# Slot weights split by ACT and by POOL in halves, the seventh batch's stored from ACT's queue, g loaded later, the stores of w_out's rows spread out

## The chip, the cores and the metric

The kernel runs on one core of one Trainium2 chip. The core has five engines with a queue each: PE (matrix products), ACT (functions, copies out of PSUM), DVE (vector work), POOL (vector work, SBUF only) and SP (here it only issues DMAs; ACT issues one too). Each takes its instructions strictly in order. The metric is the device time of one execution in microseconds, and lower is better: the median of the runs of before is 1417.61 us (1417.1 to 1418.57).

## What is computed

Three layers follow one another on x of shape (8, 3072, 256), all in float32: a spectral layer per batch, a mixture with soft slots over all 24576 tokens, and a SoLU block.

```python
X = np.fft.rfft(x, axis=1)
Yr = Xr @ w_r - Xi @ w_i + b_r                  # Yi likewise
Yr = np.sign(Yr) * np.maximum(np.abs(Yr) - lam, 0.0)
y = np.fft.irfft(Yr + 1j * Yi, n=3072, axis=1)

logits = y @ phi                                # 32 slots
d = softmax over the tokens;  c = softmax over the slots
slot_input = d.T @ y
slot_out[e] = np.maximum(slot_input[e] @ w1[e], 0.0) @ w2[e]
x2 = c @ slot_out

h = x2 @ w_in
solu = h * softmax(h)
ln = (solu - mean) / np.sqrt(var + 1e-6) * g_ln
out = ln @ w_out
```

w_in and w_out arrive as float64; the kernel decodes their 64-bit words itself.

## The kernel before

**First phase (0 to about 612 us).** `phase1` works batch by batch, the batches counted here from 1 to 8 (b = 0 to 7 in the code). A batch is 12 steps (`for i in range(B * NT)`, 96 in all, about 6 us each). A step holds one or two `stage1` (a product over 96 rows; its input is split into a high part by ACT, L237, and a low part by POOL, L238), one `stage2` (`xps`), one `mix` (`pb`, `pa`, then three DVE operations, the last of them L345, and a subtraction on POOL, L346) and one `st_transpose` (`sps`). Between them run the small operations of the batch before, which turn its spectrum into logits and softmax weights: `qt`, `qtr`, `e2`, `r_x`, `inv1`, `ltr` (which writes the logits to `lg_sb`, L459), `maxt`, `maxb`, `fwd1`, `dtr`, `d_x`, `fwd2`, `slots`.

**What sets the order.** A heap of delayed calls: `after(n, f, ...)` runs f n calls of `tick()` later (four ticks to a step). The numbers stand in the table `LAG`. What a call issues goes to the in-order queues at that place.

**Slot weights.** `csoft` to `c_x` make the weights c of a batch, `ct_sb` (96 x 1024, transposed by DVE at L536). `c_out` splits them: POOL copies the high part to `ct_h` (L551), then subtracts to get the low part in place in `ct_sb` (L552). `c_store` (L557) sends both to `c_dram` from SP's queue. The second phase reads them back. Batch 8 is stored unsplit, from ACT's queue (L548). `ct_sb` and the next batch's `lg_sb` share one buffer (tag `sc`), so `ltr` of batch b+1 has to wait until `ct_sb` of batch b has been stored.

**Decoding.** `dec_step` runs once a step from i = 2 on, with one small piece of work each time: a load of a raw block, eight DVE operations on it (L668 to L675), then for w_in one store to `win_dram`, for w_out a scaling by g on ACT (`dec_scale`, L698) and in one more step all the stores of the block's rows (`dec_rows`: 2 stores for the first two blocks, 8 for the last two). `load_g` closes the list and loads w_out back as `wo`.

**End of the first phase.** When batch 8's last `qt` is due, the buffers of the loop are released and `load_w` puts 15 loads of 512 KB (`wt`, w1 and w2) and one of 1 MB (`wi`) into SP's queue (L115, L123, L1200). Then the rest of the heap runs: `qt` to `slots` of batch 8, and `c_store` of batch 7.

**Second phase (from about 612 us).** `phase2` first computes the slots' outputs (`ph`, `h1`, `po`, `psl`, `pg`), then 192 tiles of 128 tokens, bounded by PE.

**DMA semaphores.** Each DMA has one of eight semaphores, in turn over both queues (`DMAHW0` to `DMAHW7` in the rows below); a DMA waits until the DMA that had its semaphore before has landed. So eight are under way at most.

Of the kernel before, what the change touches and what calls it, by code (L numbers as in the profile page):

```python
# [8 lines left out]
F32 = mybir.dt.float32  # L9
# [4 lines left out]
AF = mybir.ActivationFunctionType  # L14
# [6 lines left out]

LAG = dict(
    csoft_last=5, csoft2_last=4, csoft3_last=4, c_x_last=12, head=4, split0=3, load_x=3, a_out=0, qt=5, qtr=3, e2=3, r_x=2, inv1=3, mx=0, ltr=1, maxt=2, maxb=4,
    dsub=0, dexp=2, csoft=5, fwd1=4, rescale=3, rexp=3, csoft2=3, csoft3=5, c_x=4, c_out=1, c_store=5, dtr=3, d_x=3, fwd2=4,
    sums4=0, slots=1, sums=4,
)

# [8 lines left out]
def kernel(  # L36
# [112 lines left out]
    def phase1(pl: ExitStack, pr_: ExitStack):  # L149
# [39 lines left out]
        def after(dq, fn, *a):  # L189
            heapq.heappush(heap, (now[0] + dq, now[1], fn, a))  # L190
            now[1] += 1
# [353 lines left out]
        def c_out(b, ct):  # L545
            f = ct.rearrange("p n j -> p (n j)")
            if b == B - 1:
                ACT.dma_start(out=c_dram[b, 0].rearrange("h s x -> (h s) x"), in_=f.bitcast(F32))  # L548
                return
            ch = sm_p.tile([96, 1024], F32R, name="ct_h", tag="c_sb")  # L550
            POOL.tensor_copy(out=ch, in_=f.bitcast(F32))  # L551
            POOL.tensor_tensor(out=f, in0=f.bitcast(F32), in1=ch.bitcast(F32), op=ALU.subtract)  # L552
            after(LAG["c_store"], c_store, b, ch, f)

        def c_store(b, ch, f):
            for k, z in enumerate((ch, f)):
                SP.dma_start(out=c_dram[b, k].rearrange("h s x -> (h s) x"), in_=z.bitcast(F32))  # L557

        def fwd1(b, h):
            if h == 0:  # L560
# [96 lines left out]
        def decode(src, dst, k):  # L657
            z = g_p.tile([128, 2048], I32, name="dec", tag="wo")
            raw, a, c = z[:, 0:1024].bitcast(I64), z[:, 1024:1536], z[:, 1536:2048]
            m = g_p.tile([128, 512], I32, name="dm", tag="dm")  # L660
            v = z[:, 0:1024].rearrange("p (n two) -> p n two", two=2)
            hi = v[:, :, 1]
            lo = z[:, 0:1024].bitcast(U32).rearrange("p (n two) -> p n two", two=2)[:, :, 0]
            r = raw if len(src.shape) == 2 else raw.rearrange("p (k d) -> p k d", k=2)
            SP.dma_start(out=r, in_=src)
            f = a.bitcast(F32) if len(src.shape) == 2 else a.bitcast(F32).rearrange("p (k d) -> p k d", k=2)
            dec_ops.extend([
                lambda: DVE.tensor_scalar(out=a, in0=hi, scalar1=3, scalar2=0x7FFFFFF8, op0=ALU.logical_shift_left, op1=ALU.bitwise_and),  # L668
                lambda: DVE.scalar_tensor_tensor(out=a, in0=hi, scalar=_s32(0x80000000), in1=a, op0=ALU.bitwise_and, op1=ALU.bitwise_or),
                lambda: DVE.tensor_scalar(out=c, in0=hi, scalar1=0x7FF00000, scalar2=None, op0=ALU.bitwise_and),  # L670
                lambda: DVE.tensor_scalar(out=m, in0=c, scalar1=float(0x38100000), scalar2=-1.0, op0=ALU.is_ge, op1=ALU.mult),
                lambda: DVE.scalar_tensor_tensor(out=a, in0=a, scalar=0x40000000, in1=m, op0=ALU.bitwise_xor, op1=ALU.bitwise_and),
                lambda: DVE.tensor_scalar(out=c, in0=a, scalar1=_s32(0xFF800000), scalar2=None, op0=ALU.bitwise_and),
                lambda: DVE.scalar_tensor_tensor(out=c.bitcast(F32), in0=lo, scalar=2.0**-52, in1=c.bitcast(F32), op0=ALU.mult, op1=ALU.mult),
                lambda: DVE.tensor_tensor(out=a.bitcast(F32), in0=c.bitcast(F32), in1=a.bitcast(F32), op=ALU.add),  # L675
            ])
            if k < 0:
                dec_ops.append(lambda: dec_out(dst, f))
            else:
                dec_ops.append(lambda: dec_scale(f, k))  # L680
                dec_ops.append(lambda: dec_rows(f, k))

        def dec_step():
            if dec_ops:
                dec_ops.pop(0)()
            elif decs:
                decode(*decs.pop(0))
                if not decs:
                    dec_ops.append(load_g)

# [6 lines left out]
            for n in range(2):  # L697
                ACT.activation(out=f[:, n, :], in_=f[:, n, :], func=AF.Copy, scale=gl[:, k + n:k + n + 1])  # L698

        def dec_rows(f, k):  # L700
            for n in range(k, k + 2):
                if n < MA:
                    SP.dma_start(out=wout_dram[128 * n:128 * n + 128], in_=f[:, n - k, :])
                    continue
                v = wout_dram[128 * MA:1024].rearrange("(i b c) d -> b c i d", b=4, c=MB)
                for c in range(4):
                    SP.dma_start(out=v[n - MA, c], in_=f[32 * c:32 * c + 32, n - k, :])


        dft = sm_p.tile([96, 96], F32, name="dft", tag="qt_sb", bufs=2)  # L710
# [13 lines left out]
        def weights():  # L724
# [28 lines left out]
            26: (f_sb[:, 16:32, :], c_f[:, 16:32, :]),  # L753
            30: (w2_sb, c_w2),
            31: (sel, c_sel),
            33: (gl, g_ln.rearrange("(k p) -> p k", p=128)),
        }

        def load_const(o, i):
# [48 lines left out]
        for i in range(B * NT):  # L808
# [3 lines left out]
            tick()  # L812
            if i + 1 < B * NT:
                stage2(*divmod(i + 1, NT))
                if i > 1:
                    dec_step()
                if t % 2 == 0:
                    k = i // 2 + 2
                    bb, r = divmod(k, 6)
# [504 lines left out]
```

## Time and profile before

| | us |
|---|---|
| median of 3 runs | 1417.61 (1417.1 to 1418.57) |
| the profiled execution, device time | 1420.87 |
| its span, first to last instruction | 1419.1 |
| PE busy in the span | 1332.3 (94%) |
| DVE, ACT, POOL busy | 1219.3, 1040.8, 938.6 |
| mean granted PE clock | 0.975 |

The span is 1.8 us shorter than the profiled execution, and that execution is 3.3 us above the median of the runs. The page cuts the span into 40 slices: PE is busy 9 tenths or more in nearly all of them, except in the first slice and around 600 to 700 us. The averages over the span say little: the first phase, the passage at its end and the second phase have different limits.

### The profile page before, as it was taken

The numbers are of one execution on the slowest core, as the hardware profiler recorded it, in microseconds if no ns is written. First come the engines' busy times: TensorE is split into PE (matmuls) and PEld (weight loads), VectorE is DVE, ScalarE is ACT, GpSimd is POOL, SyncE is SP. The second block draws the span as 40 slices with busy tenths as digits, with TensorE's granted clock in tenths as the row PEclk, the third lists the DMA queues.
The fourth block names the chain that finished last, engine by engine and source line by source line (L and its number), as shares of the span: only waits on it lengthen the run. The fifth ranks groups of instructions, "written<-read, shape, count | busy, mean of one in ns | idle before, by whom it ended". The sixth has DMA issues, their size and how long they took to land.

```text
span 1419.1 us, 28550 instructions
## 1 busy us (share of the span) xinstructions
PE 1332.3 (94%) x10012; PEld 1133.4 (80%) x10012; DVE 1219.3 (86%) x1885; ACT 1040.8 (73%) x1999; POOL 938.6 (66%) x963
## 2 busy tenths in 40 slices
PE   6999999999999898937699999999999999999998
PEld 3888888888888787714588888888888888888787
DVE  6767989898988798815799999999999999999985
ACT  5557565657565664413599999999999999999886
POOL 5546575757574743301278878788787887879996
PEclk8899999999999999968799999999999999999999
DMA  9965364737273653274256665666656665566552
GB/s 271 291 177 169 112 194 120 212 101 208 85 208 101 190 179 105 88 283 132 81 186 207 199 189 187 200 208 198 189 189 198 206 202 187 189 198 206 167 177 83
DMA packets 207774, 250.84 MB, mean 177 GB/s; under 512 B 15536, under 2 KB 148400, under 8 KB 207632
## 3 DMA queue, kind: packets, MB, share of 16 engines
q1 hardware_dynamic: 207520, 248.63, 56.3%
q8 instruction: 80, 1.31, 0.4%
q14 instruction: 62, 0.51, 0.1%
q10 hardware_dynamic: 112, 0.39, 0.1%
HBM read 141.09 MB, written 107.87 MB: 175 GB/s over the span
## 4 chain that ended last, share of the span: by engine, by line
PE 67%; DVE 11%; POOL 9%; DMA 5%; issue 4%; ACT 2%; SPq 1%; POOLq 0%; DVEq 0%; ACTq 0%
PE po L89 33%; PE pb L89 6%; PE hps L89 6%; PE pu L92 5%; PE pm L89 4%; PE s L89 4%; PE xps L89 4%; DMA xc<-in_x_dram 3%; PE pa L89 3%; PE sps L92 2%; POOL x L238 2%; POOL ul L1080 1%; DMA c_dram<-ct_sb 1%; DVE yb L343 1%; DVE dm_sb L591 1%
## 5 line engine op out<-in xcount | busy, mean ns | idle before, releaser
L89 PE MATMUL po<-gw,uh 128*128 128x512 f32 x1536 | 407.1, 406 | 3.8 <-POOL uh L1079 3.7
L89 PEld LDWEIGHTS po<-gw,uh 128*128 128x128 f32 x1536 | 274.5, 189 | 57.5 <-POOL uh L1079 6.4
L346 POOL TENSOR_TENSOR s<-yb,s 128x512 f32<-128x512 f32 x95 | 132.0, 1389 | 205.3 <-DVE s L345 186.1
L998 DVE TENSOR_REDUCE st<-hps 128x1 f32<-128x1024 f32 x192 | 235.1, 1225 | 29.8 <-PE hps L89 10.4
L1080 POOL TENSOR_TENSOR ul<-t,uh 128x512 fp32r<-128x512 f32 x189 | 244.8, 1295 | 15.2
L1013 DVE SCALAR_TENSOR_TENSOR u<-hps,e 128x1024 f32<-128x1024 f32 x192 | 233.2, 1214 | 1.3 <-ACT e L1005 1.3
L89 PEld LDWEIGHTS po<-gw,ul 128*128 128x128 f32 x1536 | 207.4, 188 | 17.7
L1088 ACT ACTIVATE sq<-u,st 128x1024 f32<-128x1024 f32 x192 | 219.5, 1143 | 0.0
L1005 ACT ACTIVATE e<-hps,st 128x1024 f32<-128x1024 f32 x192 | 214.2, 1116 | 2.9 <-DVE st L998 2.9
L89 PE MATMUL po<-gw,ul 128*128 128x256 f32 x1536 | 210.4, 279 | 0.0
L1079 POOL CAST uh<-t 128x512 fp32r<-128x512 f32 x189 | 116.0, 614 | 135.6 <-DMA t<-td 102.3
L238 POOL TENSOR_TENSOR x<-xc,x 96x512 fp32r<-96x512 f32 x120 | 165.3, 1385 | 38.0 <-ACT x L237 36.0
L1061 ACT ACTIVATE uh<-pu 128x512 fp32r<-128x512 f32 x195 | 116.8, 599 | 66.8 <-PE pu L92 56.6
L1129 ACT ACTIVATE osb<-po,st 128x512 f32<-128x512 f32 x192 | 130.7, 681 | 9.6 <-PE po L89 6.9
L1070 DVE TENSOR_TENSOR ul<-pu,uh 128x512 fp32r<-128x512 f32 x195 | 133.6, 686 | 3.6 <-ACT uh L1061 3.6
L1042 DVE STREAM_TRANSPOSE tb<-u 128x512 f32<-128x512 f32 x189 | 132.6, 702 | 0.0
L264 ACT ACTIVATE asb<-s 96x512 f32<-96x512 f32 x112 | 66.7, 595 | 80.7 <-PE s L89 80.7
L89 PE MATMUL s<-x,df_h 96*96 96x512 f32 x240 | 105.2, 440 | 17.7 <-POOL x L238 7.0
L92 PEld LDWEIGHTS pu<-ident,u 128*128 128x128 f32 x768 | 96.5, 141 | 26.0 <-issue 0.8
L92 PE MATMUL pu<-ident,u 128*128 128x128 f32 x768 | 116.6, 275 | 0.0
L89 PE MATMUL hps<-gst,ct 128*128 128x512 f32 x336 | 106.8, 400 | 10.0 <-DVE u L1013 8.6
L1136 POOL TENSOR_TENSOR os<-osb 128x1024 f32<-128x1024 f32 x47 | 113.4, 2413 | 0.0
(205 smaller groups left out, 2593.1 us busy)
## 6 DMA issues: line engine op xcount, KB each, us to landing
td<-tb SPq DMA_DIRECT2D x189, 256.0 KB, 2.1
t<-td SPq DMA_DIRECT2D x189, 256.0 KB, 3.0
apt<-ad SPq DMA_DIRECT2D x96, 256.0 KB, 3.9
out_dram<-os SPq DMA_DIRECT2D x47, 512.0 KB, 3.7
xc<-in_x_dram SPq DMA_DIRECT2D x56, 384.0 KB, 4.0
ad<-asb SPq DMA_DIRECT2D x56, 384.0 KB, 3.6
ct<-c_dram SPq DMA_DIRECT2D x96, 128.0 KB, 3.4
wt<-in_moe_w_dram SPq DMA_DIRECT2D x21, 512.0 KB, 8.5
```

The source lines that it names most:

```text
L89: PE.matmul(out=out, lhsT=lhsT, rhs=rhs, start=start, stop=stop)
L92: PE.transpose(out=out, in_=in_, identity=ident[0:k, 0:k])
L238: POOL.tensor_tensor(out=lo, in0=t, in1=hi.bitcast(F32), op=ALU.subtract)
L346: (DVE if (b, t) == (B - 1, NT - 1) else POOL).tensor_tensor(out=s, in0=yb, in1=s, op=ALU.subtract)
L998: DVE.tensor_reduce(out=st[:, 0, k:k + 1], in_=hps[i], op=ALU.min, axis=AX.X)
L1005: ACT.activation(out=e, in_=hps[i], func=AF.Exp, bias=st[:, 0, k:k + 1], scale=-1.0, accum_out=st[:, 1, k:k + 1])
L1013: DVE.scalar_tensor_tensor(out=u, in0=hps.pop(i), scalar=1.0, in1=et.pop(i), op0=ALU.mult, op1=ALU.mult, accum_out=st[:, 2, k:k + 1])
L1042: DVE.transpose(out=t, in_=v)
L1070: DVE.tensor_tensor(out=ul[:, z, :], in0=ut.pop((i, n)), in1=uht[i][0][:, z, :].bitcast(F32), op=ALU.subtract)
L1080: POOL.tensor_tensor(out=ul[:, MA:8, :].rearrange("p c (a j) -> p c a j", a=4), in0=v, in1=w.bitcast(F32), op=ALU.subtract)
L1088: ACT.activation(out=sq, in_=ut.pop(i), func=AF.Square, bias=st[:, 2, k:k + 1], scale=-float(DFF), accum_out=st[:, 3, k:k + 1])
L1129: ACT.activation(out=o[:, k], in_=pot.pop(i), func=AF.Copy, scale=stt[j][:, 4, k:k + 1])
```

## The change

`c_out` moves the copy of the high part from POOL to ACT, one tick later (`c_out` 1 to 2). The subtraction is cut into two halves of 512 columns, two and four ticks after that (`c_lo`), and the stores come three ticks behind the second half. The stores of batch 7 are issued by ACT instead of SP. g (`gl`) is no longer loaded among the early constants but when the last block of w_in is taken up. `dec_rows` does one row block or half of one at a time, so the 20 row stores of w_out lie in 12 steps instead of 4; `dec_step` starts at i = 0 instead of 2.

```diff
-    ... c_out=1, c_store=5, ...
+    ... c_out=2, c_lo=2, c_store=3, ...
...
-            POOL.tensor_copy(out=ch, in_=f.bitcast(F32))
-            POOL.tensor_tensor(out=f, in0=f.bitcast(F32), in1=ch.bitcast(F32), op=ALU.subtract)
-            after(LAG["c_store"], c_store, b, ch, f)
+            ACT.activation(out=ch, in_=f.bitcast(F32), func=AF.Copy)
+            after(LAG["c_lo"], c_lo, b, ch, f, 0)
+            after(LAG["c_lo"] + 2, c_lo, b, ch, f, 1)
+
+        def c_lo(b, ch, f, z):
+            z_ = slice(512 * z, 512 * z + 512)
+            POOL.tensor_tensor(out=f[:, z_], in0=f[:, z_].bitcast(F32), in1=ch[:, z_].bitcast(F32), op=ALU.subtract)
+            if z:
+                after(LAG["c_store"], c_store, b, ch, f)
...
-                SP.dma_start(out=c_dram[b, k].rearrange("h s x -> (h s) x"), in_=z.bitcast(F32))
+                (ACT if b == B - 2 else SP).dma_start(out=c_dram[b, k].rearrange("h s x -> (h s) x"), in_=z.bitcast(F32))
...
-                dec_ops.append(lambda: dec_rows(f, k))
+                for n in range(k, k + 2):
+                    for q in range(0, 4, 2 if n >= MA else 4):
+                        dec_ops.append(lambda n=n, q=q: dec_rows(f, k, n, q))
...
                 decode(*decs.pop(0))
+                if len(decs) == 4:
+                    SP.dma_start(out=gl, in_=g_ln.rearrange("(k p) -> p k", p=128))
...
-            33: (gl, g_ln.rearrange("(k p) -> p k", p=128)),
...
-                if i > 1:
-                    dec_step()
+                dec_step()
```

ACT's queue at the end of the first phase, before. Names are out<-in; in brackets stand the semaphores that the instruction waits for. `qt_sb`, `q_sb`, `r_sb`, `lt_sb`, `lg_sb` are batch 8's.

```order
L397 ACTIVATE q_sb<-pm 128x256 [waits PE_49]
L358 ACTIVATE st<-sps 128x512 [waits PE_49] x2
L413 ACTIVATE r_sb<-pm 128x256 [waits PE_49]
L385 ACTIVATE qt_sb<-pm 128x2x2x64 [waits PE_49]
L397 ACTIVATE q_sb<-pm 128x256 [waits PE_49]
L413 ACTIVATE r_sb<-pm 128x256 [waits PE_49]
L440 ACTIVATE lt_sb<-pm 128x384 [waits PE_49] x2
L459 ACTIVATE lg_sb<-pm 96x512 [waits DVE_49,DMAHW3_49,PE_49,Pool_49]
```

The same place of ACT's queue now.

```order
L397 ACTIVATE q_sb<-pm 128x256 [waits PE_49]
L551 ACTIVATE ct_h<-ct_sb 96x1024 [waits DVE_49,Pool_49]
L358 ACTIVATE st<-sps 128x512 [waits PE_49] x2
L413 ACTIVATE r_sb<-pm 128x256 [waits PE_49]
L385 ACTIVATE qt_sb<-pm 128x2x2x64 [waits PE_49]
L563 DMA c_dram<-ct_h 96x1024 [waits DMAHW3_49,Activation_49]
L563 DMA c_dram<-ct_sb 96x1024 [waits DMAHW5_49,Pool_49]
L397 ACTIVATE q_sb<-pm 128x256 [waits PE_49]
L413 ACTIVATE r_sb<-pm 128x256 [waits PE_49]
L440 ACTIVATE lt_sb<-pm 128x384 [waits PE_49] x2
L459 ACTIVATE lg_sb<-pm 96x512 [waits DMAHW5_49,PE_49]
```

The copy and the two stores of batch 7 now stand in ACT's queue ahead of batch 8's `q_sb`, and `lg_sb` waits for the second of these stores.

SP's queue in the same stretch, before: the end of the loads of `load_w`, then the stores.

```order
L123 DMA wt<-in_moe_w_dram 128x4x256 [waits DMAHW7_49]
L123 DMA wt<-in_moe_w_dram 128x4x256 [waits DMAHW0_49]
L1200 DMA wi<-win_dram 128x2x1024 [waits DMAHW1_49]
L557 DMA c_dram<-ct_h 96x1024 [waits DMAHW2_49,Pool_49]
L557 DMA c_dram<-ct_sb 96x1024 [waits DMAHW3_49,Pool_49]
L123 DMA ws<-in_moe_w_dram 128x2x256 [waits DMAHW4_49,PE_49]
```

SP's queue now, from the first load of `load_w`; the semaphores 3 and 5 that are missing between 2, 4 and 6 went to the two stores on ACT.

```order
L115 DMA wt<-in_moe_w_dram 128x1024 [waits DVE_49,PE_49,DMAHW2_49,Activation_49,Pool_49]
L115 DMA wt<-in_moe_w_dram 128x1024 [waits DMAHW4_49]
L115 DMA wt<-in_moe_w_dram 128x1024 [waits DMAHW6_49]
L115 DMA wt<-in_moe_w_dram 128x1024 [waits DMAHW7_49]
L115 DMA wt<-in_moe_w_dram 128x1024 [waits DMAHW0_49]
L115 DMA wt<-in_moe_w_dram 128x1024 [waits DMAHW1_49]
L115 DMA wt<-in_moe_w_dram 128x1024 [waits DMAHW2_49]
L115 DMA wt<-in_moe_w_dram 128x1024 [waits DMAHW3_49]
L115 DMA wt<-in_moe_w_dram 128x1024 [waits DMAHW4_49]
L115 DMA wt<-in_moe_w_dram 128x1024 [waits DMAHW5_49]
```

Of the loads, the eighth now waits for the landing of the first store, the tenth for that of the second.

POOL's queue where batch 1's weights are split, before (the same in batches 2 to 5).

```order
L346 TENSOR_TENSOR s<-yb,s 128x512
L238 TENSOR_TENSOR x_2298<-xc,x_2298 96x512
L551 CAST ct_h<-ct_sb 96x1024
L552 TENSOR_TENSOR ct_sb<-ct_sb,ct_h 96x1024
L238 TENSOR_TENSOR x_2329<-xc,x_2329 96x512
L346 TENSOR_TENSOR s<-yb,s 128x512
L238 TENSOR_TENSOR x_2386<-xc,x_2386 96x512
```

POOL's queue there now.

```order
L346 TENSOR_TENSOR s<-yb,s 128x512
L238 TENSOR_TENSOR x_2299<-xc,x_2299 96x512
L238 TENSOR_TENSOR x_2327<-xc,x_2327 96x512
L346 TENSOR_TENSOR s<-yb,s 128x512
L238 TENSOR_TENSOR x_2386<-xc,x_2386 96x512
L557 TENSOR_TENSOR ct_sb<-ct_sb,ct_h 96x512
L238 TENSOR_TENSOR x_2413<-xc,x_2413 96x512
L557 TENSOR_TENSOR ct_sb<-ct_sb,ct_h 96x512
```

The copy is gone from POOL, and the halves of the subtraction stand one input split (L238) apart, behind two of them that they stood ahead of. For batches 6 and 7 no L238 is left there, and the two halves follow each other directly.

## Rows read from the trace of the kernel before

**Rows 1.** Windows: stretch, us, busy time of each engine, PEclk, DMA share, GB/s.
```profile
200.00:250.00 50.00, 48.66 (x519) 41.24 (x518) 45.73 (x83) 30.73 (x69) 29.16 (x22) 1.00 0.42 123
...
600.00:640.00 40.00, 14.15 (x138) 9.95 (x136) 10.35 (x14) 5.67 (x12) 5.00 (x4) 0.70 0.77 278
...
620.00:625.00 5.00, 0.00 (x0) 0.00 (x0) 0.00 (x0) 0.00 (x0) 0.06 (x1) 0.82 1.03 413
...
635.00:640.00 5.00, 0.40 (x2) 0.14 (x2) 0.42 (x2) 1.08 (x2) 0.00 (x0) 0.50 0.54 217
```

**Rows 2.** Waits of PE, 30 to 610 us: in total, times, longest.
```profile
PE s L89 <- POOL x L238: 5.3, 7, 1.3
...
PE s L89 <- ACT asb L264: 1.9, 3, 1.1
```

**Rows 3.** Chain of waits around the end of the first phase: start, us, what.
```profile
626.75 1.42 SPq L1200
...
629.02 9.37 DMA c_dram<-ct_sb
```

**Rows 4.** Timeline from batch 7's split to the slots: start, us, instruction [idle <-releaser].
```profile
602.66 1.03 POOL L551 CAST ct_h<-ct_sb 96x1024 fp32r<-96x1024 f32 x1 [1.35 <-DVE ct_sb L536]
...
603.78 2.34 POOL L552 TENSOR_TENSOR ct_sb<-ct_sb,ct_h 96x1024 fp32r<-96x1024 f32 x1
603.88 2.52 DVE L345 TENSOR_SCALAR s<-yb 128x512 f32<-128x512 f32 x1
...
611.15 0.38 ACT L385 ACTIVATE qt_sb<-pm 128x256 f32<-128x256 f32 x1 [1.51 <-PE pm L89]
611.25 5.30 SPq L115 DMA_DIRECT2D wt<-in_moe_w_dram  x10
...
612.70 0.39 ACT L397 ACTIVATE q_sb<-pm 128x256 f32<-128x256 f32 x1 [1.17 <-PE pm L92]
...
616.57 1.53 PE L89 MATMUL pm<-ft_sb,r_sb 128*32 128x96 f32 x64 [1.44 <-DVE r_sb L425]
...
618.03 1.30 PE L92 MATMUL pm<-ident,lt_sb 128*96 128x128 f32 x8
...
638.49 1.08 ACT L459 ACTIVATE lg_sb<-pm 96x512 f32<-96x512 f32 x2 [19.85 <-DMA c_dram<-ct_sb]
...
642.57 2.79 PE L89 MATMUL pm<-f_sb,d_sb 96*32 96x96 f32 x64 [1.73 <-ACT d_sb L496]
...
658.26 0.35 ACTq L548 DMA_DIRECT2D c_dram<-ct_sb  x1
```

**Rows 5.** Timeline, the releaser of the slots' first layer.
```profile
664.92 1.09 ACT L894 ACTIVATE h<-ph 128x512 f32<-128x512 f32 x2 [2.62 <-DMA c_dram<-ct_sb]
```

**Rows 6.** DMA packets, MB, share (q1 SP, q10 ACT) at 658, 661, 662 us, 1 us each.
```profile
q1 hardware_dynamic: 300, 0.29, 94.3%
...
q10 hardware_dynamic: 19, 0.08, 18.9%
...
q10 hardware_dynamic: 73, 0.25, 62.2%
```

**Rows 7.** Timeline behind the split of batch 2's weights.
```profile
248.28 1.46 POOL L238 TENSOR_TENSOR x<-xc,x 96x512 fp32r<-96x512 f32 x1
...
248.52 2.74 DVE L316 TENSOR_TENSOR sl<-xsum,sh 128x256 fp32r<-128x256 f32 x1
...
249.69 1.28 POOL L346 TENSOR_TENSOR s<-yb,s 128x512 f32<-128x512 f32 x1
...
249.79 0.47 PE L89 MATMUL s<-x,df_h 96*96 96x512 f32 x1 [0.67 <-POOL x L238]
```

**Rows 8.** Timeline around the eight row stores of w_out's third block.
```profile
473.33 5.89 SPq L707 DMA_DIRECT2D wout_dram<-dec  x8
...
484.14 0.63 ACT L237 ACTIVATE x<-xc 96x512 fp32r<-96x512 f32 x1 [2.89 <-DMA xc<-in_x_dram]
```

**Rows 9.** Timeline: a decoding operation on DVE near the end of batch 7's turn.
```profile
534.78 0.69 DVE L675 TENSOR_TENSOR dec<-dec 128x512 f32<-128x512 f32 x1
```

More of the change, by code (lines that the diff above doesn't have):

```diff
@@ L23 @@
     csoft_last=5, csoft2_last=4, csoft3_last=4, c_x_last=12, head=4, split0=3, load_x=3, a_out=0, qt=5, qtr=3, e2=3, r_x=2, inv1=3, mx=0, ltr=1, maxt=2, maxb=4,
-    dsub=0, dexp=2, csoft=5, fwd1=4, rescale=3, rexp=3, csoft2=3, csoft3=5, c_x=4, c_out=1, c_store=5, dtr=3, d_x=3, fwd2=4,
+    dsub=0, dexp=2, csoft=5, fwd1=4, rescale=3, rexp=3, csoft2=3, csoft3=5, c_x=4, c_out=2, c_lo=2, c_store=3, dtr=3, d_x=3, fwd2=4,
     sums4=0, slots=1, sums=4,
@@ L698, in dec_scale, with dec_rows @@
                 ACT.activation(out=f[:, n, :], in_=f[:, n, :], func=AF.Copy, scale=gl[:, k + n:k + n + 1])
[L700 to L707, printed above, removed]
+        def dec_rows(f, k, n, c):
+            if n < MA:
+                SP.dma_start(out=wout_dram[128 * n:128 * n + 128], in_=f[:, n - k, :])
+                return
+            v = wout_dram[128 * MA:1024].rearrange("(i b c) d -> b c i d", b=4, c=MB)
+            for c in (c, c + 1):
+                SP.dma_start(out=v[n - MA, c], in_=f[32 * c:32 * c + 32, n - k, :])
         dft = sm_p.tile([96, 96], F32, name="dft", tag="qt_sb", bufs=2)
```

## The prediction

> **What bounds the kernel now.** I read the busy time by stretch first. Where PE is busy throughout, only shorter work on PE helps, and the change takes nothing from PE; it can pay only where PE waits. The largest such place is the end of the first phase: in 600 to 640 us PE is busy for 14.15 of 40 us [rows 1]. The chain of waits through that stretch runs over SP's queue (L1200, the load of wi) and ends in the DMA c_dram<-ct_sb, issued at 629.02 and 9.37 us long [rows 3]. The timeline names who waited: ACT's `lg_sb` of batch 8 sat idle for 19.85 us for that store and started at 638.49, although PE had begun its transposes at 618.03 [rows 4]. `lg_sb` shares its buffer with batch 7's `ct_sb`. That `ct_sb` had been finished by POOL at 603.78 + 2.34 = 606.1 [rows 4], but its store stood in SP's queue behind 15 loads of 512 KB and one of 1 MB, which begin at 611.25 [rows 4]. In 620 to 625 the engines stand still (0.06 us on POOL) and the DMA engines move 413 GB/s [rows 1].
>
> The second place is small and repeated. In 30 to 610 us PE waits 5.3 us in 7 waits for POOL's L238 and 1.9 us in 3 waits for ACT's asb [rows 2]. Behind batch 2's split, L238 comes late because POOL has the copy and the subtraction ahead of it, and PE waits 0.67 us [rows 7].
>
> **The change, part by part.** The sum is made against the profiled execution, 1420.87 us (span 1419.1 us and 1.8 around it); that is 3.3 us above the median of the runs, and I carry the difference over as it is.
>
> *Store of batch 7 on ACT's queue.* The order shows both stores right behind batch 8's second `qt_sb`. That one ends at 611.15 + 0.38 = 611.5; an issue on ACT takes 0.35 us [rows 4], so both are out by 612.3, before ACT is wanted for `q_sb` at 612.70. Their inputs are ready: ACT's copy can start when POOL's did, at 602.66, and takes about 1.08 us, by the two activations of half that size at 638.49; POOL's two halves together cost its 2.34 us, so 606.1 again. The semaphores 3 and 5 that the stores wait for belong to the ws loads before load_w by the order, so nothing of load_w holds them up.
>
> When do they land? By 612.3 SP has issued two loads (ten take 5.30 us). Two loads are 1.05 MB and the stores 0.79 MB; at 413 GB/s [rows 1] these take 4.4 us, so 616.7 with no start-up at all. The store at 658.26 shows a start-up under load: its first packets move between 661 and 662, some 3 us after issue, while SP's queue moves 300 in one of the microseconds before [rows 6]. With that the landing is 619.7. I take 619.1, nearer to the loaded row. `lg_sb` can't start before PE's first four transposes, about 618.7. So it starts at 619.2 instead of 638.49: **-19.3 us**, bounds -19.8 and, for a store that gets its turn last, -14.5 (the first rival).
>
> *What is late next.* From `lg_sb` to the last batch's own store at 658.26 lie 19.8 us of PE, ACT, DVE and POOL in turn [rows 4]; these keep their length. The loads of load_w, wi and the two stores are the same bytes as before, and the DMA engines were done with them in 635 to 640 at a share of 0.54 [rows 1], about 637.7. Behind them come eight ws loads and the last store, 2.5 MB; at the 0.29 MB per us of [rows 6] that takes 8.6 us, to 646.3. The slots' first layer waited for that last store until 664.92 [rows 5]; moved up by 19.3 it would be 645.6. So the DMA engines take back **+0.7 us**, bounds 0 and +3.
>
> *PE's clock.* The granted clock was 0.50 in 635 to 640, the 1.2 GHz level, after PE had done nothing [rows 1]; the 64 matmuls at 642.57 took 2.79 us, and 64 of a similar kind at 616.57, 1.53 us [rows 4]. With the gap gone PE may stay at 2.4 GHz, worth -1.3 us. PE has only crumbs to do in these microseconds even so, and I take **0**.
>
> *Copy off POOL, halves behind L238 (batches 1 to 5).* POOL loses 1.03 us per batch, and by the order the two L238 that stood behind the subtraction (2.34 us at 603.78 [rows 4]) now stand ahead of it. That meets the 5.3 us of PE's waits for L238. POOL stays full in the same step and the halves delay the next L238, so I take **-4.0 us**, bounds 0 and -5.3.
>
> *Rows of w_out in twelve pieces.* Eight stores at 473.33 hold SP for 5.89 us; the next load of x is late, and ACT's L237 waits 2.89 us for it [rows 8]. That shows up in PE's 1.9 us for asb. Two stores per step have room in a step of 6 us: **-1.0 us**, bounds 0 and -1.9.
>
> *What it costs.* ACT gets the copy seven times, and it waits for DVE's transposes with `sh`, `xi` and the next `x` queued behind it; DVE and PE wait for these. In 200 to 250 us ACT is busy for 30.73 of 50 us [rows 1], so the copies mostly lie in its idle time: **+0.5 us**, at worst 1.08 us in six batches, +6.5. The decoding shifts: three DVE operations like that at 534.78, 0.69 us each [rows 9], come into batch 8's first steps, where DVE has little idle time (45.73 us busy of the same 50), and two into batch 2's end: **+1.0 us**, bounds 0 and +3.5. The first raw block is loaded a few microseconds earlier and g later: the first DVE operation on it still comes behind a whole step, and g is used some 19 steps after its new place: 0, at worst +1.5 at the start.
>
> *Batch 8's last step.* DVE's L345 started at 603.88 beside POOL's subtraction and took 2.52 us; it ended 0.3 us behind it [rows 4]. The two halves stand back to back here. In [rows 7] DVE's `sl` at 248.52 ran 2.74 us, through the whole of one POOL operation and the next (249.69 + 1.28 = 250.97): DVE didn't get in between. So **0**. The Trainium skill, "SBUF — State Buffer", section "SBUF: two separate sides", says that whoever of the two starts first has the shared port for the whole instruction. By that rule alone the gap between the halves would let DVE in 1.2 us earlier, and the time would be 1394.3; the row speaks against it, and I give it 0.1, inside the forecast.
>
> Sum: -19.3 + 0.7 - 4.0 - 1.0 + 0.5 + 1.0 = -22.1 us. That gives 1398.8 for a profiled execution and **1395.5 us** as the median.
>
> **The rivals.** *The transfer is the bound.* The stores share the 16 DMA engines with SP's loads. If they are served last, SP still stops at its eighth load, which waits for the first store: seven loads and the stores are 4.46 MB, 10.8 us, so landing at about 624 and -14.5 instead of -19.3: 1400.3 us. For it: at 658.26 the store on ACT's queue moved most of its packets (73) only in 662 to 663 [rows 6]. Against: most of what was ahead there had been issued before it; here it is two loads. Chance 0.15. The Trainium skill, "DMA: Bandwidth & Descriptors", section "Issuing engines are not separate DMA queues", says that starting DMAs from several engines only saves the issuing time. By that alone the move would save two issues of 0.35 us, and the time would be 1413.4. The trace agrees that the queues share the engines, but SP's in-order queue kept the store from being issued until 629.02 [rows 3], so I give it 0.02.
>
> *Slower: ACT stands still.* The stores now sit in ACT's queue ahead of `q_sb`. If they wait there, the whole chain `q_sb` to `lg_sb` (612.70 to 618.7, 6.0 us) waits too. Should their semaphores have been used last by loads of load_w, ACT would go on at about 637.7, `lg_sb` at 643.7, that is +5.2, and with the first phase's -3.5 and +0.7 the time is 1420.0. It decides from 635 on. Against: the order, as above. Chance 0.03.
>
> *Not what it says.* `lg_sb` before also waits for DVE and POOL; if the store were not what held it, only the first phase's -3.5 would be left: 1414.1. Against: it started 0.1 us behind the landing, 629.02 + 9.37 = 638.39. Chance 0.03.
>
> **How the numbers follow.** Forecast 0.74, spread by the bounds above from 1391 (-19.8, -1.3 by the clock, first phase -5.5) to 1400; the late store 0.15, around 1400; ACT standing still 0.03, the two cases near 1414 together 0.05; 0.03 for what I don't see. 1391 to 1402.5 leaves out less than 2 in 10. A change under 0.2% (2.8 us) can't be told from none. Faster by more than that: forecast, late store and most of the two cases near 1414, 0.96; within: 0.02; slower: 0.02.
>
> **What would show it.** In the new trace: two ACT-queue stores near 612, landing by about 619; `lg_sb` without a wait above 1 us; no stretch of 20 us in which all engines stand still; the first layer of the slots some 18 us earlier, still released by the last store; PE's waits for L238 down from 5.3 to under 1.5 us, and L237's wait behind the row stores gone. Wrong would be: `lg_sb` still waiting 5 us or more (late store), a long idle time before `q_sb` (ACT stuck), new waits of PE for ACT or DVE of more than 3 us in the first phase, or loads of w that land so late that the slots wait for them.

## The result, and the profile after

| | before | after |
|---|---|---|
| median of the runs, us | 1417.69 (1417.1 to 1418.57, 4 runs) | 1393.19 (1391.62 to 1393.42, 4 runs) |
| the profiled execution, device time, us | 1420.87 | 1393.42 |
| its span, us | 1419.1 | 1391.6 |

The ratio is 0.9824 (95% interval 0.9807 to 0.9841): 24.5 us less in the medians, where 22.1 were forecast. The profiled pair differs by 27.4 us, since before's profiled run was 3.2 us above its median and after's 0.2; below, the pair is cut into parts.

Windows of the profile after, the same stretch as the second line of [rows 1].

```profile
600.00:640.00 40.00, 31.70 (x341) 19.39 (x341) 18.92 (x32) 14.40 (x27) 4.17 (x4) 0.87 0.88 311
```

PE is busy for 31.70 of these 40 us, where it was 14.15 before. No stretch is left in which all engines stand still for more than a fraction of a us. The timeline after shows what took the place of [rows 4] and [rows 5]: ACT's queue from batch 8's second `qt_sb` to the slots' first layer.

```profile
604.02 0.38 ACT L385 ACTIVATE qt_sb<-pm 128x256 f32<-128x256 f32 x1 [1.45 <-PE pm L89]
604.08 0.38 ACTq L563 DMA_DIRECT2D c_dram<-ct_h  x1
604.56 0.38 ACTq L563 DMA_DIRECT2D c_dram<-ct_sb  x1
604.98 0.38 ACT L397 ACTIVATE q_sb<-pm 128x256 f32<-128x256 f32 x1 [0.58 <-PE pm L92]
...
611.00 1.25 ACT L459 ACTIVATE lg_sb<-pm 96x512 f32<-96x512 f32 x2
...
630.81 0.31 ACTq L548 DMA_DIRECT2D c_dram<-ct_sb  x1
637.02 1.09 ACT L901 ACTIVATE h<-ph 128x512 f32<-128x512 f32 x2 [2.18 <-PE ph L89]
```

The stores are issued right behind `qt_sb`, `q_sb` isn't held up by them, and `lg_sb` starts without a wait, 6.98 us behind `qt_sb` (611.00 - 604.02). Before it was 638.49 - 611.15 = 27.34 us: **20.4 us gained here**. The issues of the DMAs in 596 to 612 after (KB each, median us from issue to landing) show that the stores land 6.3 us after issue at most, at about 610.9, though loads of w go out beside them.

```profile
wt<-in_moe_w_dram SPq DMA_DIRECT2D x10, 512.0 KB, 8.0
c_dram<-ct_h ACTq DMA_DIRECT2D x1, 384.0 KB, 4.8
c_dram<-ct_sb ACTq DMA_DIRECT2D x1, 384.0 KB, 6.3
```

The rest lies in the first phase. PE's waits in 30 to 610 us after (us in total, times, longest), to be held against [rows 2]:

```profile
PE s L89 <- POOL x L238: 0.9, 3, 0.4
...
PE s L89 <- ACT asb L264: 0.7, 1, 0.7
```

L238's waits went from 5.3 to 0.9 us, those for `asb` from 1.9 to 0.7, and ACT's L237 waits nowhere for x in batch 7's turn (2.89 us in [rows 8]). From the first layer on nothing changed: from `h` to the end of the span it is 754.2 us before (1419.1 - 664.92) and 754.6 after.

### The profile page after: what moved, and what is told of

Read it like the earlier page. It is cut to its first block, busy times and chain, and to the rows that moved or that the text cites. A ratio compares the mean times of both kernels' runs of the same rounds, so it can differ in the third digit from the quotient of the medians.

```text
span 1391.6 us, 28564 instructions
## 1 busy us (share of the span) xinstructions
PE 1331.2 (96%) x10012; PEld 1132.7 (81%) x10012; DVE 1217.5 (87%) x1885; ACT 1045.7 (75%) x2006; POOL 929.9 (67%) x963
## 4 chain that ended last, share of the span: by engine, by line
PE 78%; DVE 9%; POOL 4%; issue 4%; DMA 2%; ACT 2%; SPq 0%; DVEq 0%; POOLq 0%; ACTq 0%
PE po L89 36%; PE pb L89 8%; PE hps L89 6%; PE pm L89 6%; PE pu L92 5%; PE s L89 5%; PE xps L89 4%; PE pa L89 3%; PE sps L92 2%; DMA xc<-in_x_dram 2%; PE pm L92 1%; POOL x L238 1%; DVE sl L316 1%; DVE yb L343 1%; DVE yb L342 1%
## 5 line engine op out<-in xcount | busy, mean ns | idle before, releaser
L346 POOL TENSOR_TENSOR s<-yb,s 128x512 f32<-128x512 f32 x95 | 132.3, 1393 | 215.9 <-DVE s L345 190.2
L238 POOL TENSOR_TENSOR x<-xc,x 96x512 fp32r<-96x512 f32 x120 | 162.7, 1365 | 32.8 <-ACT x L237 30.2
L264 ACT ACTIVATE asb<-s 96x512 f32<-96x512 f32 x112 | 66.6, 595 | 74.4 <-PE s L89 74.4
L92 PEld LDWEIGHTS pu<-ident,u 128*128 128x128 f32 x768 | 96.5, 141 | 26.1 <-issue 0.8
```

Of the source, the lines that this page charges most:

```text
L92: PE.transpose(out=out, in_=in_, identity=ident[0:k, 0:k])
L238: POOL.tensor_tensor(out=lo, in0=t, in1=hi.bitcast(F32), op=ALU.subtract)
L346: (DVE if (b, t) == (B - 1, NT - 1) else POOL).tensor_tensor(out=s, in0=yb, in1=s, op=ALU.subtract)
```

## The experiments

Each kernel's profile was cut at two marks that all of them have: the start of `xd` (L305, the first DVE operation of a batch's turn) and batch 8's second `qt_sb`. The first column of lengths is batch 1's turn (from its `xd` to that of batch 2), the second batches 2 to 8 up to that `qt_sb`, the third the passage from there to `lg_sb`. Each ratio is taken against runs of before from the same series; their medians were 1417.34 us for the four kernels below before, 1417.04 for the lines "ahead of the loads", "row stores back", "copy back" and "on DVE", and 1418.45 for "second time", "one piece", "i = 2" and the last. A difference of 1 us between lines of two series is therefore not safe.

| kernel | median, us | ratio to before, 95% | batch 1 | batches 2 to 8 | `qt_sb` to `lg_sb` |
|---|---|---|---|---|---|
| before | 1417.69 | | 58.58 | 514.62 | 27.34 |
| before, stores of batch 7 on ACT | 1398.34 | 0.9855 to 0.9885 | 55.39 | 515.06 | 6.94 |
| before, split only | 1417.40 | 0.9987 to 1.0005 | 54.53 | 515.09 | 27.24 |
| before, decoding only | 1415.99 | 0.9974 to 0.9996 | 54.39 | 512.93 | 27.17 |
| after, stores back on SP | 1412.01 | 0.9954 to 0.9980 | 54.26 | 508.68 | 27.36 |
| **after** | 1393.19 | 0.9807 to 0.9841 | 57.00 | 508.29 | 6.98 |
| after, second time | 1393.37 | 0.9806 to 0.9840 | 55.32 | 509.21 | 7.56 |
| after, stores on SP ahead of the loads | 1391.43 | 0.9807 to 0.9833 | 54.35 | 509.55 | 7.08 |
| after, row stores back in one step | 1395.41 | 0.9836 to 0.9863 | 55.50 | 512.73 | 7.55 |
| after, copy back on POOL | 1392.61 | 0.9821 to 0.9849 | 55.96 | 508.45 | 7.52 |
| after, subtraction in one piece | 1394.45 | 0.9816 to 0.9849 | 54.55 | 512.80 | 6.95 |
| after, decoding starts at i = 2 | 1396.43 | 0.9829 to 0.9865 | 53.83 | 513.17 | 6.98 |
| after, batch 7's low part on DVE | 1390.91 | 0.9800 to 0.9827 | 56.52 | 507.01 | 7.39 |
| after, low part on DVE and stores on SP first | 1390.48 | 0.9789 to 0.9830 | 56.25 | 506.03 | 6.98 |

Batch 1's turn scatters by 4.7 us, also between kernels that are alike there (58.58 and 55.39 in the first two lines). Behind it two profiles of one kernel still differ by 0.9 us (508.29 and 509.21), so a term of 1 us is at the edge of what one pair of profiles can show. The profiled run of before lost 3.2 us in batch 1 to the second line; in its timeline ACT's L237 at 79.28 us waits 4.34 us for a load of x, against 2.95 us at that place in the second line. That isn't all of what the profiled pair shows beyond the medians, though: of its 27.5 us between the spans 0.8 lie ahead of batch 2 (96.53 to 95.73), 6.3 in batches 2 to 8, 20.4 in the passage and none behind it. Where the 3 us come from stays open.

### Store of batch 7, and nothing else

```diff
-                SP.dma_start(out=c_dram[b, k]..., in_=z.bitcast(F32))
+                (ACT if b == B - 2 else SP).dma_start(out=c_dram[b, k]..., in_=z.bitcast(F32))
```

> The kernel before, and of the change only the stores of batch 7 issued by ACT. My theory: the 24.5 us of the change are 20 us from this edit (lg_sb no longer waits for a store that stands behind 16 loads on SP) and 4 us from the rest. Then this kernel is 18.5 to 21 us faster than before, about 1397.7 us, its lg_sb starts about 7 us after batch 8's second qt_sb (27.3 before, 7.0 after the change) and its first phase is as long as before's. Rival A, the transfer: without the earlier split the stores meet the loads of w, land late, and lg_sb starts 9 to 12 us after qt_sb: 1400 to 1403 us. Rival B, the gain lies mostly in the other edits: 1405 us or more.

Its median is 19.0 us below that of before in the same series (1417.34). The timeline:

```profile
606.67 0.36 ACTq L557 DMA_DIRECT2D c_dram<-ct_h  x1
607.14 0.36 ACTq L557 DMA_DIRECT2D c_dram<-ct_sb  x1
608.15 0.38 ACT L385 ACTIVATE qt_sb<-pm 128x256 f32<-128x256 f32 x1 [1.16 <-PE pm L89]
...
615.09 1.25 ACT L459 ACTIVATE lg_sb<-pm 96x512 f32<-96x512 f32 x2
```

`lg_sb` is 6.94 us behind `qt_sb`, and batches 2 to 8 take as long as before (515.06 to 514.62). The transfer isn't the bound, and the other edits aren't needed for this gain.

### The change without it

```diff
-                (ACT if b == B - 2 else SP).dma_start(...)
+                SP.dma_start(...)
```

> The changed kernel with one edit undone: batch 7's stores are issued by SP again, behind the loads of w. My theory: the wait of lg_sb for the store (some 20 us) is back, and only the first phase's gain is left: 3 to 5 us faster than before, about 1413.5 us. The profiled pair showed 7 us gained by batch 8's second qt_sb; if the medians gain as much, it is 1410.5 us. Rival: the earlier split lets the store land early even from SP's queue: 1395 to 1400 us.

1412.01 us, 5.3 below before. The wait is back at its full length:

```profile
629.69 1.08 ACT L459 ACTIVATE lg_sb<-pm 96x512 f32<-96x512 f32 x2 [20.50 <-DMA c_dram<-ct_sb]
```

So 5.3 us are the first phase's, 1.8 more than the prediction's -3.5. The store alone and the rest alone (19.0 + 5.3 = 24.3) make up the 24.5.

### Engine or place in the queue

The changed kernel, with batch 7's stores on SP, issued before the buffers of the loop are released and `load_w` is called.

```diff
-                (ACT if b == B - 2 else SP).dma_start(...)
+                SP.dma_start(...)
...
+        while any(a[2] in (c_out, c_lo, c_store) for a in heap):
+            z = min(a for a in heap if a[2] in (c_out, c_lo, c_store))
+            heap.remove(z)
+            heapq.heapify(heap)
+            z[2](*z[3])
         pr_.close()
```

> The changed kernel, but batch 7's two stores on SP's queue again, this time ahead of the loads of w instead of behind them. It tells whether the 20 us come from the engine that issues the stores or from their place ahead of the loads. My theory, the place: lg_sb starts 7 us after batch 8's second qt_sb, as with ACT's queue, and the time is that of the changed kernel within 1 us, about 1393 us. Rival, the engine (a second queue gets its share of the transfers where SP's queue doesn't): lg_sb waits for the store again, 1400 us or more. Were the landing of the stores the limit in the changed kernel (it lies about half a us ahead of lg_sb there), this kernel, which can issue them some 4 us earlier, would be faster by up to 0.5 us.

SP's queue, and `lg_sb`:

```profile
594.88 0.33 SPq L563 DMA_DIRECT2D c_dram<-ct_h  x1
597.61 0.33 SPq L563 DMA_DIRECT2D c_dram<-ct_sb  x1
602.00 5.13 SPq L115 DMA_DIRECT2D wt<-in_moe_w_dram  x10
...
609.04 1.11 ACT L459 ACTIVATE lg_sb<-pm 96x512 f32<-96x512 f32 x2 [0.21 <-PE pm L92]
```

The place ahead of the loads is what counts: from SP's own queue `lg_sb` comes 7.08 us behind `qt_sb`, as from ACT's. The median is 1.8 us lower than after's, more than I expected, but the intervals overlap; measured from before in the same series it is 25.6 us, where after had 24.5 and 25.1, so 0.5 to 1.1 us of it may be real. The profile has the difference behind `lg_sb`, where I had not looked for it: 630 to 635 us, after first and this kernel second.

```profile
630.00:635.00 5.00, 5.00 (x48) 1.44 (x46) 2.90 (x2) 1.91 (x1) 0.00 (x0) 1.00 1.08 365
```

```profile
630.00:635.00 5.00, 5.00 (x50) 1.47 (x43) 1.57 (x3) 3.00 (x3) 0.00 (x0) 1.00 0.38 133
```

Its first layer in the timeline:

```profile
633.18 1.08 ACT L906 ACTIVATE h<-ph 128x512 f32<-128x512 f32 x2 [0.44 <-PE ph L89]
```

The DMA engines are still full after (share 1.08) and mostly done here (0.38), since the 0.79 MB of stores moved at a place where the DMA engines stand idle after (a share of 0.02 in 598 to 602). `h` follows the last store (L548) by 4.5 us instead of 6.2. It also starts before PE's `ph` group would end (627.78 + 7.08 = 634.86): `h` needs a part of `ph` only. What held it shows in the landings of L548 (issued at 630.81 after and at 628.71 here):

```profile
c_dram<-ct_sb ACTq DMA_DIRECT2D x1, 384.0 KB, 6.1
...
c_dram<-ct_sb ACTq DMA_DIRECT2D x1, 384.0 KB, 4.4
```

So L548 lands at 636.9 after and at 633.1 here, and `h` starts 0.1 us behind that both times; in all 14 profiles of this study the distance is 0.1 us. After's `h` at 637.02 was held by that landing, as before, though the profile names `ph`.

### The split alone, the decoding alone

```diff
-            POOL.tensor_copy(out=ch, ...)
-            POOL.tensor_tensor(out=f, ...)
-            after(LAG["c_store"], c_store, b, ch, f)
+            ACT.activation(out=ch, ..., func=AF.Copy)
+            after(LAG["c_lo"], c_lo, b, ch, f, 0)
+            after(LAG["c_lo"] + 2, c_lo, b, ch, f, 1)
```

> The kernel before, and of the change only the split of the slot weights: the high part copied by ACT, the low part by POOL in two halves, stores from SP. My theory, with the term of the prediction: PE's waits for POOL's L238 in the first phase go from 5.3 us to about 1 us, ACT's copies cost at most 1 us: 2 to 4 us faster than before, about 1414.5 us. Rival A: ACT's copies hold up asb, x and sh and give it all back: within 1 us of before. Rival B: the first phase's gain of the whole change is from the decoding edits: this one changes nothing, and the other one 4 us.

The second kernel has instead `gl` late, `dec_rows` in pieces, and `dec_step` from i = 0.

> The kernel before, and of the change only the decoding: g loaded late, the row stores of w_out in twelve pieces, and the first step two steps earlier. My theory: the waits behind the eight row stores go (1 us), the three decoding operations that move into batch 8's first steps take some of it back: 0 to 2 us faster than before, about 1416.5 us. Together with the split it should make up what the changed kernel with SP's stores gains. Rival: the decoding edits carry the first phase's gain: 3 to 5 us faster, 1413.5 us. Slower than before by over 1 us if the moved DVE operations hold up PE.

My numbers fell for the split. Alone it gives nothing (1417.40 to 1417.34), and the decoding 1.35 us, together 5.3. The intervals are wide (0.6 to 3.7 us for the decoding, 2.8 to 6.5 for both); the marks say the same more firmly, with 515.09, 512.93 and 508.68 us for batches 2 to 8. PE's waits show that L238's wait went as expected; another grew. The split alone:

```profile
PE s L89 <- ACT asb L264: 3.8, 2, 2.8
...
PE s L89 <- POOL x L238: 0.8, 3, 0.3
```

Its longest lies in batch 7's turn. SP's queue and ACT's timeline there, near the place of the 2.89 us in [rows 8], and the window behind that wait:

```profile
475.89 0.46 SPq L671 DMA_DIRECT2D dec<-in_moe_w_out_dram  x1
476.40 1.34 SPq L220 DMA_DIRECT2D xc<-in_x_dram  x1
...
484.82 0.63 ACT L237 ACTIVATE x<-xc 96x512 fp32r<-96x512 f32 x1 [3.75 <-DMA xc<-in_x_dram]
...
488.00:492.00 4.00, 4.00 (x19) 3.50 (x20) 3.86 (x7) 2.61 (x6) 2.48 (x2) 0.59 0.36 98
```

The load of x that comes late isn't the one right behind the eight row stores (issued at 471.17, landed 4.0 us later, no wait) but the next one. It stands right behind the load of the next raw block (512 KB), which follows the row stores by one step when these are issued together, and it lands 8.3 us after issue. With the row stores in pieces, that raw block is loaded some steps later (at 490.79 in the kernel with both). Part of what PE gains ahead of the load it waits for at it: in batch 7's turn its waits come to 3.7 us instead of 4.1. Behind the wait of 2.8 us its granted clock is 0.59 in 488 to 492, and it is busy for 72.70 us of the turn instead of 71.39. Over batches 2 to 8 the split takes 2.6 us off PE's waits and adds 3.1 to its busy time. No run tells how much of this the clock makes. The turn (`xd` of batch 7 to that of batch 8) takes 75.5 and 76.7 us in the first two kernels, 76.4 with the split alone, 72.7 with the decoding alone and 71.7 with both. Batch 5's turn shows as much of a gain that only both edits give: 74.4 and 74.1, 74.6, 75.2, and 73.3 with both. There I didn't trace why the two single edits cost up to 1 us and both together gain 1.

### Row stores back in one step

```diff
-                for n in range(k, k + 2):
-                    for q in range(0, 4, 2 if n >= MA else 4):
-                        dec_ops.append(lambda n=n, q=q: dec_rows(f, k, n, q))
+                dec_ops.append(lambda: [dec_rows(f, k, n, q)
+                    for n in range(k, k + 2) for q in range(0, 4, 2 if n >= MA else 4)])
```

> The changed kernel with one edit undone: all stores of a decoded block of w_out are issued in one step again (up to eight in a row on SP). By the prediction's term this costs 1.0 us. By the traces of the split alone and of the decoding alone, where batch 7's turn takes 76.4 and 72.7 us (before 75.5 to 76.7, with both 71.7), it is more: the row stores hold SP, the next load of x is late, and what the split gains in batch 7 is lost behind it. My theory now: batch 7's turn is back at 75.5 to 76.5 us and the kernel is 3.5 to 5 us slower than the changed one, about 1397.3 us. Rival, that the late load of g or the start two steps earlier did it: 1393 to 1394 us.

2.0 to 2.2 us slower than after by the medians (2.9 to 3.4 by the distances to before in each series), less than expected, and not in batch 7: with eight pieces fewer the decoding ends earlier, and the eight stores stand elsewhere. In the profile batches 2 to 8 take 3.5 to 4.4 us longer, most of it in batch 5 (75.7 us to 73.3). SP's queue there, ACT's next wait for x, and the KB and the us from issue to landing of that load here and of the one at its place after (issued at 330.85):

```profile
329.04 0.48 SPq L671 DMA_DIRECT2D dec<-in_moe_w_out_dram  x1
329.57 1.66 SPq L220 DMA_DIRECT2D xc<-in_x_dram  x1
...
338.35 0.63 ACT L237 ACTIVATE x<-xc 96x512 fp32r<-96x512 f32 x1 [3.26 <-DMA xc<-in_x_dram]
...
xc<-in_x_dram SPq DMA_DIRECT2D x1, 384.0 KB, 8.7
...
xc<-in_x_dram SPq DMA_DIRECT2D x1, 384.0 KB, 5.6
```

The two row stores of this block aren't what makes the load of x late: they have landed 3 us before it is issued, and it is issued at nearly the same point of the turn as after (22.7 and 22.6 us in). It stands again right behind the load of the next raw block, where after has a single row store of 128 KB, and takes 3.1 us longer to land. So the cost isn't quite the one that the prediction named (stores that hold SP): issued together, the row stores bring the next raw block's load forward, and where that meets a load of x differs from batch to batch.

### Which part of the split pays

First the copy alone goes back to POOL.

```diff
-            ACT.activation(out=ch, in_=f.bitcast(F32), func=AF.Copy)
+            POOL.tensor_copy(out=ch, in_=f.bitcast(F32))
```

> The changed kernel with one edit undone: the high part of the slot weights is copied by POOL again, at the same place, and the halves stay. My theory: POOL's 1.03 us per batch come back in a step in which it is full, and PE waits for L238 again by 0.5 to 1 us in each of five batches; in batch 8's last step POOL is late by 1 us more. 3 to 5 us slower than the changed kernel, about 1397 us. Rival: the halves behind L238 are what pays, not the engine of the copy: within 1 us of it, 1393 to 1394 us.

The rival held: 1392.61 us, no slower than after. PE's waits for L238 come to 1.0 us in 3 waits, as after. So at its new place the copy costs nothing on POOL either; what it cost at its old one, ahead of the subtraction and an L238, no run tells. Then the subtraction in one piece, at the place of the first half; the stores keep theirs.

```diff
-            after(LAG["c_lo"] + 2, c_lo, b, ch, f, 1)
...
-            z_ = slice(512 * z, 512 * z + 512)
+            z_ = slice(0, 1024)
```

> The changed kernel with one edit undone: POOL makes the low part in one instruction of 1024 columns (2.34 us in the trace of before), at the place of the first half, one input split (L238) further back than the copy stood. The run with POOL's copy showed no difference (1392.6), so the copy's engine isn't what pays. If the cutting in halves pays, the second L238 behind it is late by 1.2 us and PE waits for L238 in batches 1 to 5 again: 2 to 4 us slower, about 1396 us. Rival, that only the place behind the two L238 pays: within 1 us of the changed kernel, 1393 us; and I hold this for the likelier, since L238's waits came from the two that stood behind the subtraction.

Here I held the wrong one for likelier:

```profile
PE s L89 <- POOL x L238: 5.5, 7, 1.3
```

The waits are all back (before 5.3 in 7), and batches 2 to 8 take 3.6 to 4.5 us longer in the profile. The medians show 1.1 us (1394.45 to 1393.37 in the same series), so the size is open between 1 and 4. That the place of the first half doesn't remove L238's waits without the cut is shown; one piece at the place of the second half wasn't tried.

### Start of the decoding

```diff
-                dec_step()
+                if i > 1:
+                    dec_step()
```

> The changed kernel, but decoding starts at i = 2 again, as before. In the traces the first step of batch 1 on DVE (xd) starts at 37.7 to 38.0 us where decoding starts at 2 (three traces) and at 38.1 to 39.4 where it starts at 0 (seven). If the early start costs that, this kernel is 0.7 us faster than the changed one, its xd at 37.9 us; if it is the scatter of the loads at the start, the time is the same within 0.5 us.

Both of my cases fell: it is 3.1 us *slower*. The row stores in pieces make the decoding eight steps longer; the early start takes two of them back out of the end, where they cost. Two places show it. The first is the passage from batch 7's turn to batch 8's; SP's queue there, starting at `i = 2`, and PE:

```profile
505.05 0.40 SPq L671 DMA_DIRECT2D dec<-in_moe_w_out_dram  x1
505.49 4.28 SPq L115 DMA_DIRECT2D wt<-in_moe_w_dram  x6
509.81 6.12 SPq L275 DMA_DIRECT2D apt<-ad  x4
...
521.33 0.71 PE L89 MATMUL xps<-d_sb,apt 128*128 128x128 f32 x4 [1.46 <-DMA apt<-ad]
```

The last raw block's load stands right ahead of six loads of w and of the loads `apt` (the input of `stage2`), and PE waits 1.8 us for two of these (0.31 and 1.46). After, in its second profile, that raw block is loaded 13.6 us ahead of the loads of w (491.10 and 504.65). No other profile of this study has a wait of PE for `apt` of 0.3 us or more behind batch 1. The second place is batch 8's `r_sb`:

```profile
546.07 0.68 DVE L680 SCALAR_TENSOR_TENSOR dec<-dec 128x512 f32<-128x512 uint32 x1
...
550.02 0.68 DVE L681 TENSOR_TENSOR dec<-dec 128x512 f32<-128x512 f32 x1
...
554.96 1.51 PE L89 MATMUL pm<-ft_sb,r_sb 128*32 128x96 f32 x32 [3.92 <-DVE r_sb L425]
```

Two decoding operations stand ahead of DVE's transposes of `r_sb`, and PE waits 3.92 us instead of 3.20. Together batches 7 and 8 take 2.9 us longer than in after's second profile (153.06 to 150.11), and PE's waits make up 2.0 of that. The rest is longer busy time. I don't put it down to the longer wait and the clock behind it, for the granted clock differs also behind equal waits. With the copy back on POOL and with the subtraction in one piece PE waits 3.20 us for `r_sb`, up to 554.42 and 554.66; the windows 554 to 558 of the two:

```profile
554.00:558.00 4.00, 3.58 (x80) 3.13 (x81) 1.98 (x4) 1.89 (x4) 0.46 (x1) 1.00 0.02 4
...
554.00:558.00 4.00, 3.33 (x60) 2.73 (x64) 1.49 (x3) 1.09 (x2) 0.72 (x1) 0.50 0.00 0
```

The granted clock is 1.00 (2.4 GHz) in the first and 0.50 (1.2 GHz) in the second.

### DVE beside POOL in batch 8's last step

After, POOL's two halves of batch 7 stand beside DVE's last L345 and L346, for which PE waits:

```profile
596.90 2.66 POOL L557 TENSOR_TENSOR ct_sb<-ct_sb,ct_h 96x512 fp32r<-96x512 f32 x2 [2.44 <-ACT ct_h L551]
597.02 1.42 DVE L345 TENSOR_SCALAR s<-yb 128x512 f32<-128x512 f32 x1
598.48 1.63 DVE L346 TENSOR_TENSOR s<-yb,s 128x512 f32<-128x512 f32 x1
...
600.26 1.04 PE L92 MATMUL sps<-ident,s 128*128 128x128 f32 x4 [3.98 <-DVE s L346]
```

The test gives batch 7's low part to DVE, which has nothing to do behind L346.

```diff
-            POOL.tensor_tensor(out=f[:, z_], ...)
+            (DVE if b == B - 2 else POOL).tensor_tensor(out=f[:, z_], ...)
```

> The changed kernel, but the low part of batch 7's slot weights is made by DVE, behind batch 8's last L346, instead of by POOL beside it. In the changed kernel DVE's L345 and L346 take 1.42 and 1.63 us there, beside POOL's two halves; elsewhere 0.43 and about 0.65 us. My theory, that the two engines take turns at SBUF: with POOL still, L345 and L346 take 0.43 and 0.65 us, PE's wait for them falls from 4.0 to about 2 us, and the kernel is 2.0 us faster than the changed one, about 1391.2 us. Rival: L345 and L346 are slow for another reason (their wait for PE's product or the type of their operands): no difference, 1393.2 us. The DVE work that is added (about 1.3 us) lies in a stretch in which DVE stands idle for 6.5 us.

```profile
597.17 0.43 DVE L345 TENSOR_SCALAR s<-yb 128x512 f32<-128x512 f32 x1
597.63 0.69 DVE L346 TENSOR_TENSOR s<-yb,s 128x512 f32<-128x512 f32 x1
598.24 1.28 DVE L557 TENSOR_TENSOR ct_sb<-ct_sb,ct_h 96x512 fp32r<-96x512 f32 x2
598.47 0.63 PE L92 MATMUL sps<-ident,s 128*128 128x128 f32 x4 [2.04 <-DVE s L346]
```

As expected: with POOL still, the two take 0.43 and 0.69 us and PE waits 2.04 us. The median is 1390.91, 2.3 us below after's; measured from before in the same series it is 26.1 us, 1.0 to 1.6 more than after, so the forecast of 2.0 is right within what the runs can tell.

### The best of both

The same edit together with the stores on SP ahead of the loads.

> The changed kernel with both edits that the runs point to: the low part of batch 7 made by DVE behind L346, and its two stores on SP's queue ahead of the loads of w. The first alone gave 1390.9, the second 1391.4 us. L345 and L346 take 0.43 and 0.69 us, the stores are issued some 4 us before the loads, and the gains (2.0 us of PE's wait; 0 to 1 us from the transfers) add up: 2 to 3 us faster than the changed kernel in this call, about 1390.5 us. If the stores' earlier place gives nothing, it is the same as the DVE edit alone, 2 us faster.

1390.48 us, 2.9 us below after in the same series (1393.37) and 0.4 below the DVE edit alone. It is the fastest kernel of this study, though one of its runs took 1394.57, and against the DVE edit alone there is no difference that the runs can tell. Its profile shows that the earlier stores did bring `h` forward (25.1 us behind `lg_sb`, with the DVE edit alone 26.2), but from `h` to the end of the span it takes 755.8 us instead of 753.5. PE waits there for a load of w that the other profiles don't wait for; that is 0.9 of the 2.3 us:

```profile
643.94 1.05 PE L89 MATMUL po<-ws,h1t 128*32 128x256 f32 x10 [0.94 <-DMA ws<-in_moe_w_dram]
```

## Why the prediction was right, point by point

| step | predicted | measured |
|---|---|---|
| store of batch 7 on ACT | -19.3 | -19.0 alone; 20.4 by the marks of the profiled pair |
| what is late next | +0.7 | -0.4 (`slt` to `h`: 7.87 before, 7.44 after) |
| PE's clock | 0 | 0 |
| copy off POOL, halves | -4.0 | 0 alone; 1.1 when the halves are undone |
| rows in twelve pieces, decoding shift | -1.0 and +1.0 | -1.35 alone; 2 when the rows are undone, 3 when the early start is |
| first phase together | -3.5 | -5.3 |
| sum | -22.1 | -24.5 |

**The store** was right in mechanism and size. The second landing was estimated at 6.8 us behind the end of its issue (619.1 from 612.3); it was 6.0 (610.9 from 604.56 + 0.38). The rival with the late transfer fell with that, and so did those in which ACT stands still (`q_sb` waited 0.58 us) or `lg_sb` waits for something else. By the rule of the Trainium skill that the prediction weighed ("DMA: Bandwidth & Descriptors", "Issuing engines are not separate DMA queues") the time would have been 1413.4. The runs agree with the rule as far as it goes: SP's queue does as well as ACT's when the stores stand ahead of the loads (7.08 and 6.98 us). What the estimate of 1413.4 left out is that the store behind the loads wasn't issued until 629.02 [rows 3].

**What is late next.** By the landings above the last store still sets the first layer, as the step said, but with 0.4 us gained, not 0.7 lost. That transfers could be moved *ahead* of the loads, into idle time of the DMA engines, wasn't in the prediction.

**PE's clock.** The 64 matmuls of `fwd1` took 2.79 us again. The granted clock in 616 to 620, where they end, is 0.50, the 1.2 GHz level, although the long gap is gone; in the 4 us ahead PE was busy for 1.74:

```profile
615.09 2.79 PE L89 MATMUL pm<-f_sb,d_sb 96*32 96x96 f32 x64 [1.74 <-ACT d_sb L496]
...
616.00:620.00 4.00, 4.00 (x57) 3.64 (x50) 0.62 (x1) 1.85 (x5) 1.91 (x1) 0.50 1.03 409
```

**Copy and halves** is the step that failed in its reason. It subtracted PE's waits for L238 as if each were worth its length. Alone, the same waits went by 4.5 us for no gain: 1.9 us came back as longer waits for `asb`, above all at a load of x behind the next raw block's, and PE's busy time grew by 3.1, part of it at a lower granted clock. The step also counted POOL's 1.03 us, which were worth nothing at the copy's new place. Behind the prediction's "1.0 us" for **the rows** stood the wait of 2.89 us in [rows 8], of which I took only the part that PE showed as a wait for `asb`, and which I put down to stores that hold SP; that the stores in one step also bring the next raw block's load forward, into the way of a load of x, wasn't in it. In batch 7's turn the two terms should have been one: they remove two waits on the same path, and the gain needs both. **The decoding shift** has the right sign for batch 8 (78.4 us with the decoding alone, 77.9 and 77.6 in the first two kernels); that the two steps at the start buy 3 us back wasn't seen. So the first phase's -3.5 is near the -5.3 partly by luck: none of its terms was measured at its size.

**Batch 8's last step** came out as forecast (PE's wait 4.1 before, 3.98 after) for a partly wrong reason. From [rows 7] I took that DVE wouldn't get in between two POOL operations. It did: L345 ended 0.2 us behind the first half (596.90 + 1.33 = 598.23). That is as the rule of the Trainium skill's "SBUF — State Buffer", "SBUF: two separate sides", would have it, by which the one that starts first has the shared port for the whole instruction. But L346 then met the second half, and took 1.63 instead of 0.69 us. So the gap let one operation through and held the next. Why `sl` in [rows 7] ran through two POOL operations stays open.

## What to carry to other kernels

A store that frees a buffer must stand ahead of a batch of loads in the issuing queue, whichever engine issues it; look for the queue's place, not for a faster transfer. Two waits on the same path aren't two terms: ask of each what PE would wait for next if it were gone, and test edits alone and together. When a load is late, look at what stands right ahead of it in its queue and when that landed, before a store further ahead is blamed. Before a term of 1 us is read from one pair of profiles, cut both at marks and leave out the part that scatters.

## What the runs showed of the hardware that was not expected

An engine can be slowed to a third by its neighbour without any wait in the trace: DVE's L345 took 1.42 us beside POOL's subtraction and 0.43 us without it, and only the duration tells. Batch 1's turn, in which the DMA engines are nearly full (a share of 0.8 to 1.0 in most windows up to 80 us), differed by 3.2 us between profiles of kernels with the same instructions there. And behind an equal wait of PE, 3.20 us, the granted clock of 554 to 558 us was 1.00 in one profile and 0.50 in another.
